# Retention attention and a routed MoE on one core: drain moved behind the last gather, raw rows in the weights' buffers, expert 5's rows turned by DMA

## The chip, the core and the metric

The kernel runs on one NeuronCore of a Trainium2 chip. A core has TensorE (PE in the profile; PEld is its weight load), VectorE (DVE), ScalarE (ACT), GpSimd (POOL) and SyncE (SP, which here only issues DMAs). The time is device microseconds of one launch. Before the change it is 446.14 us, the median of three runs (442.72 to 449.33).

## What is computed

Eight batches of eight heads, 576 positions, head size 64, go through a causal retention (attention without softmax, with a decay per head). The result, 4608 rows of 512, goes through a noisy top-2 router and eight experts.

```python
# q, k, v: [8, 8, 576, 64]
scores = 1/sqrt(64) * q @ k.transpose(0, 1, 3, 2)
Dmat = where(rel >= 0, gamma[h] ** rel, 0)
x = ((scores * Dmat) @ v)            # laid out as [4608, 512]
noisy = x @ w_gate + log1p(exp(x @ w_noise)) * noise
top2, top2_w = two largest of noisy, softmax over the two
for e in range(8):                   # w1 [8, 512, 1024], w2 [8, 1024, 512]
    rows = those with e among their two
    out[rows] += top2_w * (relu(x[rows] @ w1[e]) @ w2[e])
```

## The kernel before

**A planner writes the order.** The kernel does not issue instructions as it goes. Each piece of work is an `op` of the class `Plan` (L55) with the engine or engines that may do it, a cost, a priority, the buffers that it reads and writes, and `after`, other ops that it has to follow. When all ops are recorded, `run` simulates the engines with these costs and so decides the order of each engine's instructions and which buffer of a class each tile gets; then it emits them. Costs and priorities set nothing but this order. On the chip each engine, and each DMA queue (SP's, and POOL's for gathers and scatters), goes through its list in order.

**Buffers.** They come in classes (L253 on): `big`, ten of [128, 1024] in float32; `half`, 21 of half that size; `xg`, 24 for gathered rows; `W`, three for the weights of an expert in bf16; `ps`, the eight banks of PSUM. Streams within a class (`att` for attention, `exp` for weights, `xt` for turned rows) have quotas.

**Attention.** A unit u is one batch and four heads, 16 units in all; units 4n to 4n+3 make a batch pair. `load` (L437) brings raw k, v and q rows in by SP DMAs into `big` buffers: q per unit, k and v per batch. `cast` (L475) turns them into bf16 (k on ACT or DVE, q with its decay at L498, v at L505), `tr` turns tiles by TensorE (L521), `scores`, `states` and `out_` do the retention, `tail` the last 64 positions. `route` (L711) computes the gates of a batch pair and writes its rows with their weights to a scratch array in HBM, `xd` (L874).

**Experts.** An expert has at most 1216 rows, that is ten pieces of 128 rows (the last has 64). `weights` (L906) loads an expert: experts 0 to 2 by four POOL DMAs each that cast on the way (L914, L918), held until the loads of the units 10, 15 and 15 have landed; experts 3 to 7 by SP into `big` buffers (L928 for the first matrix, L931 for the second), from where ACT or DVE cast them into `W` (L277, L279). `fetch` (L968) gathers the rows of a piece from `xd` (L981). In the late stage each gather also waits for a recent matmul, so that gathers go at TensorE's pace. The rows have then to be turned: for experts below `CROSS` TensorE transposes them, four to a piece (L1003), and ACT or DVE copies them from PSUM; for experts from `CROSS` on, in the late stage, SP issues a DMA transpose for each piece (L993).

`up` (L1043, matmuls L1058) is the first matmul for the early tiles. In the late stage `wide` (L1071, matmuls L1084) does the first matmul of a tile interleaved with the second of the tile before (`down`, L1146; short pieces L1156); ACT applies the relu (L1067). A late expert has tiles of 512, 512 and 192 columns. `finish` (L1166) evicts a result scaled by its gate (ACT L1180, DVE L1182) and scatters it to the output by an indirect DMA on POOL's queue (L1186): in the first half of each expert's row list as a write, in the rest as an accumulating scatter. Each token has two experts, so the accumulating ones must find the writes done.

**The end.** `record` (L1210) strings it all together. Ahead of the last scatters it puts a GpSimd drain, by priority:

```python
if i == len(ts) - 1:
    pl.op("POOL", 6.0, lambda _: self.nc.gpsimd.drain(), prio=pr - 6,
          after=self.scats[i - 2][:1])
```

`overflow` (L1305) is a loop for experts with too many rows; it makes no round here.

Of the kernel before, what the change touches and what calls it, by code (L numbers as in the profile page):

```python
# [8 lines left out]
F32 = mybir.dt.float32  # L9
F16 = mybir.dt.float16  # L10
BF16 = mybir.dt.bfloat16
# [6 lines left out]
P = 128  # L18
N = 4608
NCOL = N // P  # L20
E = 8
F = 1024
DM = 512
KD = DM // P
KF = F // P
# [217 lines left out]
class Kernel:  # L243
    def __init__(self, tc, ctx, src, gates, noise, w1, w2, out, xd):
        self.tc, self.nc = tc, tc.nc
        self.src, self.gates, self.noise, self.w1, self.w2, self.out = src, gates, noise, w1, w2, out
        self.xd = xd
        nc = self.nc
        self.pl = pl = Plan()
        self.cp = ctx.enter_context(tc.tile_pool(name="fix", bufs=1))  # L250
        self.ps = ctx.enter_context(tc.tile_pool(name="ps", bufs=1, space=bass.MemoryType.PSUM))
        mk = lambda n, k, sh, dt: [(self.cp.tile(sh, dt, name=f"{n}{i}"), None) for i in range(k)]
        pl.cls("big", mk("big", 10, [P, 1024], F32), exp=4, xt=3, rt=1)  # L253
        pl.cls("half", mk("half", 21, [P, 512], F32), cs=9, exp=15, xt=3, tl=6, rt=1)
# [177 lines left out]

    def inp(self, fn, t, prio, dma):

        self.inps.append(self.pl.op("SP", 0.55, fn, w=[t], prio=prio, dma=dma, after=self.inps[-5:-4]))

    def load(self, u):  # L437
        pl, nc = self.pl, self.nc
        bp, hq, b = self.unit(u)
        d = self.u[u] = {}  # L440

        if not hq:
            self.raw = {n: [pl.buf("big", "att") for c in range(2)] for n in "kv"}
        for n in "kqv":
            if n == "q":
                t = d["rawq"] = pl.buf("big", "att")
                s = self.src[n][2 * bp + b, 4 * hq:4 * hq + 4]

                for a in range(2):
                    self.inp(lambda e, s=s, t=t, a=a: nc.sync.dma_start(  # L450
                        out=t.t[a::2].rearrange("p (h x) -> p h x", h=2),
                        in_=s[2 * a:2 * a + 2, :512].rearrange("h (p r) d -> p h (r d)", r=8)), (t, a), u, 0.72)
                continue
            d["raw" + n] = self.raw[n]
            if hq and u > 1:
                continue
            h0, nh = (4 * hq, 4) if u < 2 else (0, E)
            for c, t in enumerate(self.raw[n]):
                self.inp(lambda e, n=n, t=t, c=c: nc.sync.dma_start(
                    out=t.t[:, h0 * P:(h0 + nh) * P].rearrange("p (h x) -> p h x", h=nh),  # L460
                    in_=self.src[n][2 * bp + b, h0:h0 + nh, 256 * c:256 * c + 256].rearrange("h (p r) d -> p h (r d)", r=2)),
                    (t, hq) if u < 2 else t, u, 0.24 * nh)

    def load_tail(self, bp, prio):
        pl, nc = self.pl, self.nc
        d = self.tails[bp] = {}
        for n in "kqv":
            t = d["raw" + n] = pl.buf("half", "tl")
            for b in range(2):
                self.inp(lambda e, n=n, t=t, b=b: nc.sync.dma_start(  # L470
                    out=t.t[b * HD:(b + 1) * HD].rearrange("p (h d) -> p h d", h=E),
                    in_=self.src[n][2 * bp + b, :, 512:, :].rearrange("h s d -> s h d")),
                    (t, b), prio, 0.8)

    def cast(self, u):  # L475
        pl, nc = self.pl, self.nc
        d = self.u[u]
        hq = self.unit(u)[1]
        hs = slice(4 * hq, 4 * hq + 4)
        tab, tabq = self.fixed["tab"], self.fixed["tabq"]  # L480
        bf = lambda b: b.t.bitcast(BF16)
        kn, qb, vn = (pl.buf("half", "cs") for _ in range(3))
        rk, rq, rv = d.pop("rawk"), d.pop("rawq"), d.pop("rawv")

        def k(e, c):
            i = rk[c].t.rearrange("p (g h r d) -> p g h r d", g=2, h=4, r=2)[:, hq]
            o = bf(kn).rearrange("p (r c h d) -> p c h r d", r=2, c=2, h=4)[:, c]
            if e == "ACT":
                nc.scalar.activation(o, i, Act.Copy, scale=0.125)
            elif e == "DVE":  # L490
                nc.vector.tensor_scalar_mul(o, i, 0.125)
        for c in range(2):
            pl.op({"ACT": 0.63, "DVE": 0.43}, 0, lambda e, c=c: k(e, c), r=[(rk[c], hq)], w=[(kn, c)], prio=u, port=True)

        def q(e):
            i = rq.t.rearrange("p (h r d) -> p h r d", h=2, r=8)
            o = bf(qb).rearrange("p (r h d) -> p h r d", r=8, h=2)
            self.eng(e).tensor_tensor(o, i, tabq.t[:, 2 * hq:2 * hq + 2].unsqueeze(3).to_broadcast([P, 2, 8, HD]), Alu.mult)  # L498
        pl.op({"DVE": 1.23, "POOL": 1.91} if u > 1 else {"DVE": 1.23}, 0, q, r=[rq, tabq], w=[qb], prio=u, port=True)

        def v(e, c):
            i = rv[c].t.rearrange("p (g h r d) -> p g h r d", g=2, h=4, r=2)[:, hq]
            o = bf(vn).rearrange("p (r c h d) -> p c h r d", r=2, c=2, h=4)[:, c]
            t = tab.t[:, hs, 2 * c:2 * c + 2].unsqueeze(3).to_broadcast([P, 4, 2, HD])
            self.eng(e).tensor_tensor(o, i, t, Alu.mult)  # L505
        for c in range(2):
            pl.op({"DVE": 0.69, "POOL": 1.06}, 0, lambda e, c=c: v(e, c), r=[(rv[c], hq), tab], w=[(vn, c)], prio=u, port=True)
        d.update(kn=kn, qb=qb, vn=vn)

    def tr(self, u):  # L510
# [457 lines left out]
    def fetch(self, i, t, prio):  # L968

        pl, nc = self.pl, self.nc  # L970
        e, js, early = t
# [4 lines left out]
        for x, j in zip(xg, js):  # L976
            h, n = HPE * e + j, self.size(j)
            pace = PACE if early == 3 and i > self.ne else 0.0

            def get(_, x=x, h=h, n=n, pace=pace):  # L980
                ins = nc.gpsimd.indirect_dma_start(  # L981
                    out=x.t[:n, :], out_offset=None, in_=self.xd[:rows, :], in_offset=IOff(ap=xi.t[:n, h:h + 1], axis=0),
                    bounds_check=rows - 1, oob_is_err=False)
                if pace:
                    self.tc.add_manual_dep(ins.ins, self.mm.ins.name, mybir.DependencyInfo(
                        mybir.DependencyClass.Sync, mybir.DependencyReason.DATA), reason="gathers go at TensorE's pace")
            pl.op("POOL", 1.3, get, r=[xi] + self.xd_done[early], w=[x], prio=prio, dma=0.4, pace=pace, slack=3)
        xT = pl.buf("half" if early < 3 else "big", "xt")
        w, m, off = sum(self.size(j) for j in js), len(js) * P, self.off(js)
        xv = lambda m=m: xT.t.bitcast(BF16)[:, :KD * m].rearrange("p (k s) -> p k s", k=KD)  # L990
        if e >= CROSS and early == 3:
            for s, x in enumerate(xg):
                pl.op("SP", 0.5, lambda _, s=s, x=x, n=self.size(js[s]): nc.sync.dma_start_transpose(  # L993
                    out=xv()[:, :, off[s]:off[s] + n], in_=x.t[:n, :DM // 2].bitcast(BF16)),
                    r=[x], w=[(xT, s)], prio=prio, dma=1.1)
        for c in range(0, 0 if e >= CROSS and early == 3 else len(js), 2):
            p = self.psum("xt")
# [168 lines left out]
    def finish(self, i, t, s, prio):  # L1166
# [43 lines left out]
    def record(self):  # L1210
# [59 lines left out]
        for i in range(ne, len(ts) + 1):  # L1270
# [145 lines left out]
```

## Time and profile before

| what | value |
|---|---|
| median of three runs | 446.14 us (449.33, 442.72, 446.14) |
| profiled execution | 442.35 us |
| its span (first to last instruction) | 440.8 us |
| mean granted TensorE clock | 0.952 |
| TensorE busy | 379.5 us (86%) |
| ACT, POOL, DVE busy | 266.2, 296.9, 157.0 us |
| moved by DMA | 93.01 MB, 211 GB/s on average |
| gathers (L981), scatters (L1186) | 80 and 74 on POOL |
| TensorE transposes of gathered rows (L1003) | 240 |
| DMA transposes (L993) | 20 |

A row of the timeline gives the start, the duration, the engine, the line, the operation with output and input, and in brackets the idle time ahead of it with what ended that. A row of a window gives the busy time of PE, PEld, DVE, ACT and POOL with the count of instructions, then the granted clock of TensorE as a share of full speed, the busy share of the DMA engines and GB/s. A row of the waits gives who waited, for whom, and us in total, times and the longest. The tenths are the span in 40 slices of 11 us. Columns x elements stand behind an operation as output and input.

### The profile page before, as it was taken

The page shows a single profiled execution, that of the slowest core. Times are in us where ns is not written, and L with a number is a line of the kernel's source. Part 1 is how long each engine was busy: PE and PEld are TensorE (multiplying, and loading weights), DVE is VectorE, ACT ScalarE, POOL GpSimd, SP SyncE. Part 2 cuts the span into 40 slices and gives each one's busy share as a digit, 9 for nine tenths or more (in the row PEclk, how much of TensorE's full clock was granted, in tenths as well). Part 3 has the DMA queues.
Part 4 walks back from the last instruction along what each step waited for, and adds up shares of the span by engine and source line. Part 5 has one row for each costly group of instructions (what it writes and reads, how often), then busy time and mean ns, then how long its engine had stood idle before and what let it go on. Part 6 is the DMA issues. An engine that isn't in the chain of part 4 may idle for free. (4 is left out here: it accounts for less than half of the span.)

```text
span 440.8 us, 11068 instructions
## 1 busy us (share of the span) xinstructions
PE 379.5 (86%) x4315; PEld 243.6 (55%) x4352; DVE 157.0 (36%) x426; ACT 266.2 (60%) x458; POOL 296.9 (67%) x340
## 2 busy tenths in 40 slices
PE   2786775697699879899999799999999999999990
PEld 1675664575577657666566445555554454454450
DVE  4645689897357755101245014014113000000000
ACT  4688795855869655457657365556557555555550
POOL 8774685691888567277577577777788788562274
PEclk9999897969879889999999899999999999999996
DMA  8998999999992999964798859968779999682566
GB/s 241 311 270 192 309 252 308 321 204 210 285 273 50 246 184 202 356 230 133 226 321 317 257 170 237 292 177 238 201 168 271 204 148 150 103 101 34 66 79 103
DMA packets 94776, 93.01 MB, mean 211 GB/s; under 512 B 31615, under 2 KB 72064, under 8 KB 94722
## 3 DMA queue, kind: packets, MB, share of 16 engines
q1 hardware_dynamic: 76930, 56.83, 44.8%
q0 software_dynamic: 17792, 35.46, 39.8%
q8 instruction: 34, 0.56, 0.6%
q14 instruction: 20, 0.16, 0.1%
HBM read 72.32 MB, written 26.36 MB: 224 GB/s over the span
## 5 line engine op out<-in xcount | busy, mean ns | idle before, releaser
L1146 PE MATMUL ps<-W,half 128*128 128x512 bf16 x550 | 181.6, 381 | 3.7 <-DMA W<-in_moe_w_dram 2.5
L1084 PE MATMUL ps<-big,W 128*128 128x512 bf16 (+4 forms) x629 | 179.0, 329 | 0.8
L1067 ACT ACTIVATE half<-ps 128x512 bf16<-128x512 f32 (+5 forms) x186 | 92.9, 503 | 99.2 <-PE ps L1084 82.0
L1186 POOL DMA_INDIRECT out_dram<-half,xg x74 | 98.5, 1332 | 55.1 <-ACT half L1180 25.5
L981 POOL DMA_INDIRECT xg<-xd,xi x80 | 83.6, 1046 | 54.7 <-DMA xd<-xg 16.8
L1146 PEld LDWEIGHTS <-half 128*128 128x128 bf16 x576 | 56.0, 98 | 63.2 <-issue 3.8
L1084 PEld LDWEIGHTS <-W 128*128 128x128 bf16 x640 | 62.7, 98 | 47.2 <-issue 0.9
L1180 ACT ACTIVATE half<-ps,xg 128x512 f32<-128x512 f32 (+1 forms) x67 | 44.1, 658 | 13.7 <-PE ps L1146 10.8
L560 DVE TENSOR_TENSOR half<-ps,mask 128x512 bf16<-128x512 f32 x64 | 40.2, 679 | 15.6 <-PE ps L552 14.4
L277 ACT ACTIVATE half<-ps 128x1024 bf16<-128x1024 bf16 (+1 forms) x36 | 35.4, 999 | 15.9 <-PE ps L1003 5.9
L279 DVE CAST W<-big 128x1024 bf16<-128x1024 f32 x30 | 19.9, 719 | 55.3 <-PE ps L1156 28.7
L1182 DVE TENSOR_SCALAR half<-ps,xg 64x256 f32<-64x256 f32 (+1 forms) x15 | 9.0, 603 | 81.1 <-ACT half L1067 68.1
L505 POOL TENSOR_TENSOR half<-big,tab 128x512 bf16<-128x512 f32 x31 | 32.1, 1049 | 2.0 <-PE ps L521 1.1
L1058 PE MATMUL ps<-half,W 128*128 128x256 bf16 (+1 forms) x288 | 31.6, 267 | 2.0 <-DMA W<-in_moe_w_dram 1.7
L498 POOL TENSOR_TENSOR half<-big,tabq 128x1024 bf16<-128x1024 f32 x13 | 24.7, 1903 | 7.4 <-DMA big<-in_q_dram 4.5
L1058 PEld LDWEIGHTS <-W 128*128 128x128 bf16 x288 | 25.1, 102 | 7.0 <-DMA W<-in_moe_w_dram 2.0
L277 ACT ACTIVATE tb<-ps 64x512 bf16<-64x512 f32 x32 | 18.9, 591 | 13.4 <-PE ps L585 11.4
L277 ACT ACTIVATE xT<-ps 128x512 bf16<-128x512 f32 (+1 forms) x40 | 20.1, 555 | 7.5 <-PE ps L701 5.3
L1003 PE MATMUL ps<-ident__61,xg 128*128 128x128 bf16 (+1 forms) x240 | 19.9, 223 | 4.2 <-DMA xg<-xd,xi 4.2
L585 PE MATMUL ps<-half,half 64*64 64x64 bf16 (+2 forms) x512 | 19.6, 228 | 1.9 <-DVE half L560 1.6
L1003 PEld LDWEIGHTS <-xg 128*128 128x128 bf16 (+1 forms) x240 | 15.1, 100 | 10.7 <-DMA xg<-xd,xi 5.4
L277 ACT ACTIVATE xg<-ps 128x1024 bf16<-128x1024 bf16 (+1 forms) x20 | 17.9, 946 | 4.9 <-DMA xd<-xg 4.3
(164 smaller groups left out, 401.9 us busy)
## 6 DMA issues: line engine op xcount, KB each, us to landing
big<-in_moe_w_dram SPq DMA_DIRECT2D x40, 512.0 KB, 7.7
big<-in_q_dram SPq DMA_DIRECT2D x32, 256.0 KB, 6.6
big<-in_k_dram SPq DMA_DIRECT2D x14, 512.0 KB, 6.7
big<-in_v_dram SPq DMA_DIRECT2D x14, 512.0 KB, 8.2
W<-in_moe_w_dram POOLq DMA_DIRECT2D x12, 512.0 KB
xd<-xg SPq DMA_DIRECT2D x16, 264.0 KB, 5.7
xg<-xd,xi POOLq DMA_INDIRECT x80
out_dram<-half,xg POOLq DMA_INDIRECT x74
```

The lines of the kernel that those rows point to most:

```text
L277: self.nc.scalar.activation(out, in_, Act.Copy)
L498: self.eng(e).tensor_tensor(o, i, tabq.t[:, 2 * hq:2 * hq + 2].unsqueeze(3).to_broadcast([P, 2, 8, HD]), Alu.mult)
L505: self.eng(e).tensor_tensor(o, i, t, Alu.mult)
L560: nc.vector.tensor_tensor(S.t.bitcast(BF16).rearrange("p (h c x) -> p h c x", h=2, c=2)[:, h], p[h].t.rearrange("p (c x) -> p c x", c=2), ...
L981: ins = nc.gpsimd.indirect_dma_start(out=x.t[:n, :], out_offset=None, in_=self.xd[:rows, :], in_offset=IOff(ap=xi.t[:n, h:h + 1], axis=0), ...
L1003: nc.tensor.transpose(pv()[:, di, a:a + n], xb[:, di * P:(di + 1) * P], ident.t[:n, :n])
L1058: nc.tensor.matmul(pv()[:, f2, :], lhsT=w.t[:, o:o + P], rhs=xv()[:, di, :n], start=(di == 0), stop=(di == KD - 1))
L1067: self.nc.scalar.activation(o, i, Act.Relu)
L1084: self.mm = nc.tensor.matmul(p.t[:, :n], lhsT=w.t[:, o:o + P], rhs=xv()[:, di, :n], start=(di == 0), stop=(di == KD - 1))
L1146: self.mm = self.nc.tensor.matmul(po.t, lhsT=hv[:, c:c + P], rhs=self.W[e].t[:, o:o + DM], start=(f == 0), stop=(f == KF - 1))
L1180: nc.scalar.activation(y.t[:n, c], x, Act.Copy, scale=g()[:n])
L1186: ins = nc.gpsimd.indirect_dma_start(out=self.out[:, :], out_offset=IOff(ap=ix()[:n], axis=0), in_=y.t[:n, :], in_offset=None, bounds_chec ...
```

## The change

Four things change.

1. `CROSS` goes from 6 to 5: expert 5's ten late pieces too are turned by SP's DMA transposes, and the planner takes 2.0 instead of 0.5 for one.
2. Raw k and v rows of the batch pairs 0 and 2 go into parts of the weight buffers W1 and W2, raw q rows of the units below 8 into parts of W0, seen as float32; the rest stay in `big`, which now consists of five tiles of two. k and v of a whole batch pair share their tiles. The weights of experts 0, 1 and 2 also wait for all work on these parts.
3. The planner's cost of an accumulating scatter goes from 1.3 to 1.8.
4. The drain follows the last gather (`self.got`) by its `after`, with an earlier priority and cost 8.8 instead of 6.0.

The core of the diff:

```diff
-CROSS = 6
+CROSS = 5
...
-        pl.cls("big", mk("big", 10, [P, 1024], F32), exp=4, xt=3, rt=1)
+        bs = [self.cp.tile([P, 2, 1024], F32, name=f"big{i}") for i in range(5)]
+        pl.cls("big", [(x[:, i, :], x) for x in bs for i in range(2)], exp=4, xt=3, rt=1)
...
-        pl.cls("W", mk("W", 3, [P, KD * F + KF * DM], BF16))
+        ws = [self.cp.tile([P, KD * F + KF * DM], BF16, name=f"W{i}") for i in range(3)]
+        pl.cls("W", [(x, None) for x in ws])
+        part = lambda x, i, n: x[:, 2 * i * n:2 * i * n + 2 * n].bitcast(F32)
+        pl.cls("wkv", [(part(x, i, 2048), None) for x in ws[1:] for i in range(2)])
+        pl.cls("wq", [(part(ws[0], i, 1024), None) for i in range(4)])
...
-        if not hq:
-            self.raw = {n: [pl.buf("big", "att") for c in range(2)] for n in "kv"}
+        if u % 4 == 0:
+            self.raw = {n: [pl.buf("big", "att", 2) if bp % 2 else pl.buf("wkv", "att") for c in range(2)] for n in "kv"}
...
-                t = d["rawq"] = pl.buf("big", "att")
+                t = d["rawq"] = pl.buf("wq", "att") if u < 8 else pl.buf("big", "att")
...
-            pl.op("POOL", 1.3, get, r=[xi] + self.xd_done[early], w=[x], prio=prio, dma=0.4, pace=pace, slack=3)
+            self.got = pl.op("POOL", 1.3, get, r=[xi] + self.xd_done[early], w=[x], prio=prio, dma=0.4, pace=pace, slack=3)
...
-                pl.op("SP", 0.5, lambda _, s=s, x=x, n=self.size(js[s]): nc.sync.dma_start_transpose(
+                pl.op("SP", 2.0, lambda _, s=s, x=x, n=self.size(js[s]): nc.sync.dma_start_transpose(
...
-            self.scats.setdefault(i, []).append(pl.op("POOL", 1.3, lambda _: scat(second, True), r=[y] + src + rd,
+            self.scats.setdefault(i, []).append(pl.op("POOL", 1.8, lambda _: scat(second, True), r=[y] + src + rd,
...
-            self.weights(e, 40 + e, True, landed(u))
+            raw = (("wkv", "att"), ("wq", "att"))[e == 0]
+            self.weights(e, 40 + e, True, landed(u) + [o for b in pl.fifo[raw] for o in b.ops])
...
-                pl.op("POOL", 6.0, lambda _: self.nc.gpsimd.drain(), prio=pr - 6, after=self.scats[i - 2][:1])
+                pl.op("POOL", 8.8, lambda _: self.nc.gpsimd.drain(), prio=pr - 20, after=[self.got])
```

More of the change, by code (lines that the diff above doesn't have):

```diff
@@ L433, in inp @@
     def inp(self, fn, t, prio, dma):
-        self.inps.append(self.pl.op("SP", 0.55, fn, w=[t], prio=prio, dma=dma, after=self.inps[-5:-4]))
+        self.inps.append(self.pl.op("SP", 0.55, fn, w=t, prio=prio, dma=dma, after=self.inps[-5:-4]))
     def load(self, u):
@@ L451, in load @@
                         out=t.t[a::2].rearrange("p (h x) -> p h x", h=2),
-                        in_=s[2 * a:2 * a + 2, :512].rearrange("h (p r) d -> p h (r d)", r=8)), (t, a), u, 0.72)
+                        in_=s[2 * a:2 * a + 2, :512].rearrange("h (p r) d -> p h (r d)", r=8)), [(t, a)], u, 0.72)
                 continue
             d["raw" + n] = self.raw[n]
-            if hq and u > 1:
+            if u % 4 == 3 or bp and u % 4 == 1:
                 continue
-            h0, nh = (4 * hq, 4) if u < 2 else (0, E)
+            m = slice(u % 4 * 4, 16 if u % 4 == 2 else 8 if bp or u else 4)
             for c, t in enumerate(self.raw[n]):
[L459 to L462, printed above, removed]
+                w = [(t, x) for x in range(m.start // 4, m.stop // 4)]
+                self.inp(lambda e, n=n, t=t, c=c, m=m, bp=bp: nc.sync.dma_start(
+                    out=rows(t, m),
+                    in_=self.src[n][2 * bp:2 * bp + 2].rearrange("b h s d -> (b h) s d")[
+                        m, 256 * c:256 * c + 256].rearrange("h (p r) d -> p h (r d)", r=2)),
+                    w, u, 0.22 * (m.stop - m.start))
     def load_tail(self, bp, prio):
@@ L472, in load_tail @@
                     in_=self.src[n][2 * bp + b, :, 512:, :].rearrange("h s d -> s h d")),
-                    (t, b), prio, 0.8)
+                    [(t, b)], prio, 0.8)
     def cast(self, u):
@@ L477, in cast @@
         d = self.u[u]
-        hq = self.unit(u)[1]
+        bp, hq, bt = self.unit(u)
+        x4 = 2 * bt + hq
+        flat = lambda t: t.t.rearrange("p b x -> p (b x)") if t.n == 2 else t.t
         hs = slice(4 * hq, 4 * hq + 4)
@@ L492, in cast @@
         for c in range(2):
-            pl.op({"ACT": 0.63, "DVE": 0.43}, 0, lambda e, c=c: k(e, c), r=[(rk[c], hq)], w=[(kn, c)], prio=u, port=True)
+            pl.op({"ACT": 0.63, "DVE": 0.43}, 0, lambda e, c=c: k(e, c), r=[(rk[c], x4)], w=[(kn, c)], prio=u, port=True)
         def q(e):
@@ L506, in cast @@
         for c in range(2):
-            pl.op({"DVE": 0.69, "POOL": 1.06}, 0, lambda e, c=c: v(e, c), r=[(rv[c], hq), tab], w=[(vn, c)], prio=u, port=True)
+            pl.op({"DVE": 0.69, "POOL": 1.06}, 0, lambda e, c=c: v(e, c), r=[(rv[c], x4), tab], w=[(vn, c)], prio=u, port=True)
         d.update(kn=kn, qb=qb, vn=vn)
```

6 lines of the change are left out of this document (4 added, 2 removed).

## The prediction, made before the result

> **What bounds the kernel now.** I read the page first (busy times, slices), then windows of the span, then the waits of TensorE behind 185 us.
>
> ```profile
> span 440.8 us, 11068 instructions
> PE 379.5 (86%) x4315; PEld 243.6 (55%) x4352; DVE 157.0 (36%) x426; ACT 266.2 (60%) x458; POOL 296.9 (67%) x340
> PE   2786775697699879899999799999999999999990
> DMA  8998999999992999964798859968779999682566
> ```
>
> ```profile
> 80.00:100.00 20.00, 14.27 (x288) 11.92 (x286) 18.64 (x38) 11.95 (x21) 17.33 (x27) 0.83 1.11 259
> 180.00:200.00 20.00, 19.84 (x166) 13.72 (x168) 1.00 (x2) 11.10 (x19) 12.22 (x12) 1.00 0.77 277
> 240.00:260.00 20.00, 17.24 (x94) 8.85 (x94) 4.31 (x11) 9.66 (x19) 12.35 (x12) 0.91 0.79 261
> 400.00:420.00 20.00, 19.89 (x110) 9.76 (x110) 0.96 (x2) 10.55 (x19) 6.07 (x4) 1.00 0.35 44
> 420.00:440.80 20.80, 9.21 (x66) 5.21 (x65) 0.00 (x0) 5.40 (x13) 12.25 (x8) 0.81 0.72 96
> ```
>
> ```profile
> PE ps L1003 <- DMA xg<-xd,xi: 2.7, 1, 2.7
> ```
>
> Columns of a window: PE, PEld, DVE, ACT and POOL busy, TensorE's clock, DMA share, GB/s. There are three regimes. Up to about 180 us (attention, routing, first tiles) PE has holes while the DMA digits stand at 8 or 9: the inputs set the pace as much as any engine. From 180 to 420 us TensorE alone is the bound, 19.84 to 19.89 of 20 us, and the last fence is its only wait behind 185 us; one stretch, 240 to 260, falls to 17.24 at clock 0.91. Behind 430 us only scatters are left, on POOL. So an edit pays by fewer TensorE instructions, by closing that one hole, by a shorter end, or by earlier inputs.
>
> The profiled execution took 442.35 us, 1.55 above its span; the median of the three runs is 446.14, 3.8 more. I sum against 442.35 and add 3.8.
>
> **The drain.** POOL issues gathers and scatters in order, and the drain holds it until what it has issued is done.
>
> ```profile
> 369.88 1.05 POOL L981 DMA_INDIRECT xg<-xd,xi  x1 [0.30 <-PE ps L1156]
> 404.33 1.43 POOL L1186 DMA_INDIRECT out_dram<-half,xg  x1 [8.43 <-DVEq L1306]
> 411.26 1.54 POOL L1186 DMA_INDIRECT out_dram<-half,xg  x1 [1.79 <-ACT half L1180]
> 420.63 1.54 POOL L1186 DMA_INDIRECT out_dram<-half,xg  x1 [7.83 <-ACT half L1180]
> 431.72 1.42 POOL L1186 DMA_INDIRECT out_dram<-half,xg  x1 [0.30 <-issue]
> 433.45 1.57 POOL L1186 DMA_INDIRECT out_dram<-half,xg  x1 [0.30 <-issue]
> ```
>
> ```profile
> 413.75 0.68 ACT L1180 ACTIVATE half<-ps,xg 128x512 f32<-128x512 f32 x1
> 426.49 0.68 ACT L1180 ACTIVATE half<-ps,xg 128x512 f32<-128x512 f32 x1
> ```
>
> The bracket of the 420.63 row blames ACT, but the first eviction behind the gap was done at 414.43. The drain stood there, from 412.80 to about 420.3, 7.5 us, and the eight scatters behind it then ran back to back, 1.54+0.30 each, to 435.02. Without it the third-last scatter starts when its eviction is done, 426.49+0.68+0.30 = 427.47, the next at 429.31, the last at 431.03 (its neighbour takes 1.42+0.30) and ends at 432.60: 2.4 us sooner. The changed order puts the drain right behind the last gather and one scatter, 12 scatters from the end. In the old trace that place is the 8.43 us gap before 404.33, so 7.5 us fits there. Queued behind it are those scatters alone, no gather. The last gather itself moves later: 13 scatters from the end instead of 24; POOL has 24.7 us for 11 scatters at 1.86 and five gathers at 1.34 there, 27 us, so the drain starts some 2.5 us late, about 398, and ends about 406; by 418 the queue has caught up. Bounds: 0 (caught up too late) and -2.4; I take **-2.4**, since the gaps of 8.43 and 1.79 us together exceed the debt.
>
> **Expert 5's pieces turned by SP.** 40 of the 240 TensorE transposes go, with five PSUM copies of about 1 us on ACT or DVE, which are not the bound.
>
> ```profile
> 300.00:320.00 20.00, 2.12 (x32) 1.87 (x32) 1.00 0.78 231
> 320.00:340.00 20.00, 0.62 (x8) 0.39 (x8) 1.00 0.94 222
> DMA to landing us min/median/max: 4.1/5.2/6.0
> 326.99 0.38 PE L1084 MATMUL ps<-big,W 128*128 128x512 bf16 x1
> ```
>
> ```profile
> 247.18 0.40 PE L1003 MATMUL ps<-ident__61,xg 128*128 128x128 bf16 x4 [2.66 <-DMA xg<-xd,xi]
> 247.41 0.30 PE L1084 MATMUL ps<-big,W 128*128 128x320 bf16 x1
> ```
>
> The first two rows are windows of the transposes' line alone: expert 5's forty lie in 300 to 327, where TensorE is never idle. Four of them push the next matmul by 0.23 us (247.18 to 247.41), so ten pieces are worth 2.3 us. Bounds: -2.3, and 0 if SP delivers the pieces later than TensorE would turn them; **-2.3**, since the stage is TensorE's alone. In their place SP issues ten more DMA transposes, which land in 5.2 us (third row, of the old twenty).
>
> **Longer accumulating scatters** change the order alone: 1.8 is what the trace shows (1.54+0.30). They matter for the hole at 244:
>
> ```profile
> 239.27 1.28 POOL L981 DMA_INDIRECT xg<-xd,xi  x1 [1.23 <-PE ps L1156]
> 240.48 14.45 SPq L931 DMA_DIRECT2D big<-in_moe_w_dram  x4
> 242.11 0.30 PE L1084 MATMUL ps<-big,W 128*128 128x320 bf16 x1
> 242.46 0.30 PE L1084 MATMUL ps<-big,W 128*128 128x320 bf16 x1
> ```
>
> ```profile
> 242.00:244.00 2.00, 2.00 (x16) 1.20 (x14) 0.42 (x4) 1.20 (x3) 1.70 (x2) 1.00 0.98 365
> 248.00:250.00 2.00, 2.00 (x9) 0.90 (x8) 0.00 (x0) 1.08 (x2) 0.50 (x1) 0.63 1.09 285
> 250.00:252.00 2.00, 2.00 (x7) 0.94 (x7) 0.00 (x0) 0.74 (x2) 0.50 (x1) 0.51 0.54 162
> ```
>
> The listed order shows that the piece turned at 247.18 is the one gathered at 239.27: 7.9 us, with the weight loads beside it at 365 GB/s. The wait cost 2.66 us, and then the clock: 2x(1-0.63)+2x(1-0.51) = 1.7 us lost, 4.4 in all. How much room has each gather? I count the columns of matmuls between the one that releases a gather and its transpose, 832 columns per 0.35 us (242.11 to 242.46, one 320 and one 512 wide). Among the 15 gathers from the middle of expert 3 to the end of 4, four have under 8 us, the least 5.4, and one of the four stalled. In the changed order, where pieces are turned one by one just ahead of use, 11 of these 15 have 5.6 to 7.8 us. So the hole need not go: the pressure is wider though its worst place is milder. Bounds: -4.4 (no stall) and +8.8 (the old rate of one in four gives three); I take **0**, one stall somewhere, nearest to the one row that there is.
>
> Would a wait of 2.66 us cost any clock? The Trainium skill's "TensorE: Matmul & The Clock Gate", section "Part 1: The HAM clock gate", says that the clock halves after an idle window of about 3.4 us. By that rule the hole costs 2.7 us and not 4.4; the trace speaks against it, with 0.63 and 0.51 granted right behind the wait.
>
> **Raw rows in the weights' buffers.** The number of DMAs and their order on SP stay; buffers come free sooner.
>
> ```profile
> PE ps L521 <- POOL half L498: 3.4, 4, 1.2
> PE ps L1146 <- DMA W<-in_moe_w_dram: 2.5, 2, 1.7
> PE ps L1058 <- DMA W<-in_moe_w_dram: 1.7, 1, 1.7
> ```
>
> ```profile
> PE ps L521 <- POOL half L498: 0.5, 1, 0.5
> ```
>
> TensorE waits 3.4 us for q's casts, 0.5 of it in the first 25 us (last row, the waits of that window), where no buffer is short; 2.9 could go. But DMA stands at 1.11 in 80 to 100: rows that may start sooner need not land sooner. Against it, the weights of experts 0 to 2 now also wait for the casts out of their buffers, and TensorE already waits 2.5+1.7 for weights; these gates come after units 10 and 15 have landed, by when units 0 to 11 are long cast. Bounds: -2.9 and +4.2; I take **-1.5**, half of the gain, DMA being the cover.
>
> **Sum:** -2.4-2.3+0-1.5 = -6.2; 436.15 for the profiled execution, and with 3.8 **440.0** for the median.
>
> **Rivals.**
>
> No stall (B): the new order keeps every gather ahead. For it: the least room grows from 5.4 to 5.6 and transposes wait for one piece, not four. Another -4.4: 435.5, faster by over 2%.
>
> More stalls (C): two or three of the 11. For it: the 7.9 us landing is longer than all 11 rooms. Against it: that landing lay beside a burst of loads. +4.4 to +8.8: 444.4 to 448.8. Beside it stands the Trainium skill's "DMA: Bandwidth & Descriptors", section "Issuing engines are not separate DMA queues": DMAs of all issuers run on the same 16 engines and interleave. By that rule the ten new transposes would slow gathers too; the late gather beside SP's loads agrees.
>
> Late weights (D): +4.2 in place of -1.5 makes 445.7.
>
> Slower (E): SP's queue is in order. In the changed order the first two transposes of expert 5 stand ahead of expert 6's last four weight loads and the other eight behind. The waits of SP's queue in 260 to 335, and its rows:
>
> ```profile
> SPq L931 <- PE ps L1146: 12.6, 2, 11.1
> SPq L931 <- DVE W L279: 10.7, 3, 10.1
> ```
>
> ```profile
> 280.56 11.45 SPq L931 DMA_DIRECT2D big<-in_moe_w_dram  x3
> 315.06 4.06 SPq L993 DMA_TRANSPOSE big<-xg  x2
> 324.52 3.74 SPq L931 DMA_DIRECT2D big<-in_moe_w_dram  x4
> ```
>
> Those loads were held 11.1 and 10.1 us and ended at 292.0. If the holds return behind expert 5's first transposes and last beyond 326.99-5.2 = 321.8, TensorE waits up to 21.2 us: 461.2. Against it: expert 6's pair of 315.06 had its loads behind it with no long hold (324.52, done in 3.74), and there are 30 us of room.
>
> **Chances.** Forecast 0.36 (own range 437.5 to 443), B 0.34, C 0.14, D 0.06, E 0.10. Over 2% faster (below 437.2, about what a measurement can tell from no change) is B, 0.34; within 2% are the forecast, C and D, 0.56; slower E, 0.10. The range leaves E out and the outer ends of B and C: 431 (B with the rows' full 2.9, and 3 more of the runs' spread) to 449 (C).
>
> **What would show it.** Drain: its gap lies ahead of the 12th-last scatter, and the last scatter ends some 2.4 us behind the last eviction or less. Transposes: 200 TensorE and 30 SP ones, none of them waited for at expert 5. Gathers: the waits of TensorE behind 185 us, one of 2 to 3 us with a cold clock behind it; none is B, two or three C. Rows: the waits for q's casts fall below 3.4 while those for weights stay at 4.2. A wait of TensorE on turned pieces at expert 5 would be E. I am wrong if the stage from 180 to 420 us gains or loses anything that is not a wait for gathered rows.

## The result, and the profile after

Over 20 runs each, the changed kernel takes 440.29 us (436.12 to 445.22) against 444.38 (441.06 to 449.33) for the kernel before, a ratio of 0.9895 with a 95% interval of 0.9862 to 0.9928: 1.1% faster, a gain clear of the noise, but inside the 2% that the chances spoke of. All ratios, here and below, leave out executions that took over 1.5% more than the fastest one of the same kernel (in the run after3 below that leaves three of six). The profiled execution took 438.85 us, its span 437.2.

First the page of the changed kernel (span, busy times, the slices).

```profile
span 437.2 us, 11020 instructions
PE 378.9 (87%) x4312; PEld 240.4 (55%) x4312; DVE 161.9 (37%) x425; ACT 263.3 (60%) x450; POOL 298.1 (68%) x344
PE   2787686585989699999899898999999899999991
DMA  8997999999993999973689859459999999697586
```

The late stage, before a row of nines with one seven, now has four eights, and the DMA share from the first wide matmul to the last eviction goes from 0.77 to 0.84. To see what moved, cut both executions at three marks: the first matmul of the late stage, the end of the last eviction, the end of the last scatter. The first mark is the first start in the line of the wide matmuls (changed kernel's line numbers are 12 higher in this part of the code), here before and after:

```profile
L1084 PE MATMUL ps<-big,W x629: 243/379/474, 202.7 to 426.0; 128*128 128x512 bf16 x78, 128*128 128x192 bf16 x48, 128*128 128x384 bf16 x16, 128*128 128x448 bf16 x8
```

```profile
L1096 PE MATMUL ps<-big,W x640: 243/370/390, 199.1 to 424.6; 128*128 128x512 bf16 x80, 128*128 128x192 bf16 x48, 128*128 128x384 bf16 x16, 128*128 128x448 bf16 x8
```

The last eviction and the scatters around it, after:

```profile
427.98 0.69 ACT L1192 ACTIVATE half<-ps,xg 128x512 f32<-128x512 f32 x1 [0.92 <-ACT half L1192]
```

```profile
396.90 1.58 POOL L1198 DMA_INDIRECT out_dram<-half,xg  x1 [0.30 <-issue]
406.00 1.54 POOL L1198 DMA_INDIRECT out_dram<-half,xg  x1 [7.51 <-ACT half L1079]
429.69 1.56 POOL L1198 DMA_INDIRECT out_dram<-half,xg  x1 [0.30 <-POOLq L1319]
```

| stretch | before | after | difference |
|---|---|---|---|
| start to first wide matmul | 202.7 | 199.1 | -3.6 |
| from there to the end of the last eviction (429.99; 428.67) | 227.3 | 229.6 | +2.3 |
| from there to the end of the last scatter (435.02; 431.25) | 5.0 | 2.6 | -2.4 |
| from there to the end | 5.8 | 5.9 | +0.2 |

(Before, the last eviction started at 429.30 and took 0.69.) So there are two gains, at the start and at the end, and a loss in between. The drain is the gap of 7.51 us ahead of 406.00, behind the last gather and one scatter, as planned, and the last scatter now ends 2.6 us behind the last eviction.

The waits of TensorE in the changed kernel behind 185 us, then two rows of its waits over the whole span:

```profile
PE ps L1015 <- DMA xg<-xd,xi: 4.8, 5, 1.5
PE ps L1158 <- ACT half L1079: 2.6, 1, 2.6
```

```profile
PE ps L533 <- POOL half L510: 7.2, 5, 3.0
PE ps L1158 <- DMA W<-in_moe_w_dram: 0.2, 1, 0.2
```

One wait of 2.7 us for gathered rows has become five of up to 1.5, and there is a new one of 2.6 us for a relu on ACT. The waits for q's casts rose from 3.4 to 7.2 us, but that is no work of the change: a second profile of each kernel (before2 and after2 below) has 6.0 and 6.6. Those for the weights of the early experts fell from 4.2 to 0.2 (3.3 to nothing in the second pair).

The new wait is a short story on ACT's list (rows of ACT, then of TensorE):

```profile
346.83 0.58 ACT L1079 ACTIVATE half<-ps 128x512 bf16<-128x512 f32 x1
349.25 1.06 ACT L282 ACTIVATE W<-big 128x1024 bf16<-128x1024 f32 x1 [1.84 <-DMA big<-in_moe_w_dram]
350.21 1.07 ACT L1079 ACTIVATE half<-ps 128x512 bf16<-128x512 f32 x2
```

```profile
350.84 0.39 PE L1158 MATMUL ps<-W,half 128*128 128x512 bf16 x1 [2.61 <-ACT half L1079]
```

Between two relus (L1079) stands a cast of expert 7's weights (L282) whose load has not landed; ACT waits 1.84 us for it, casts, and only then does the relu that TensorE wants. Over the late stage ACT waits so four times, which it never did before; and the slowest weight load took 16.6 us to land instead of 11.8 (rows of the changed kernel's waits of ACT behind 195 us and of its weight loads, then of the loads before):

```profile
ACT W L282 <- DMA big<-in_moe_w_dram: 6.1, 4, 2.3
```

```profile
DMA to landing us min/median/max: 3.9/7.3/16.6
```

```profile
DMA to landing us min/median/max: 4.1/7.7/11.8
```

### The profile page after: what moved, and what is told of

It reads as the page before. It is cut to its first block, busy times and chain, and to the rows that moved or that the text cites. A ratio compares the mean times of both kernels' runs of the same rounds, so it can differ in the third digit from the quotient of the medians.

```text
span 437.2 us, 11020 instructions
## 1 busy us (share of the span) xinstructions
PE 378.9 (87%) x4312; PEld 240.4 (55%) x4312; DVE 161.9 (37%) x425; ACT 263.3 (60%) x450; POOL 298.1 (68%) x344
## 5 line engine op out<-in xcount | busy, mean ns | idle before, releaser
L1158 PE MATMUL ps<-W,half 128*128 128x512 bf16 x576 | 186.2, 379 | 2.9 <-ACT half L1079 2.6
L1096 PE MATMUL ps<-big,W 128*128 128x512 bf16 (+4 forms) x640 | 182.5, 329 | 0.0
L1079 ACT ACTIVATE half<-ps 128x512 bf16<-128x512 f32 (+5 forms) x188 | 93.5, 504 | 95.3 <-PE ps L1096 79.9
L1192 ACT ACTIVATE half<-ps,xg 128x512 f32<-128x512 f32 (+1 forms) x58 | 39.3, 678 | 12.9 <-PE ps L1158 11.6
L1194 DVE TENSOR_SCALAR half<-ps,xg 64x256 f32<-64x256 f32 (+1 forms) x24 | 14.0, 591 | 89.1 <-ACT half L1079 40.5
L282 ACT ACTIVATE half<-ps 128x1024 bf16<-128x1024 bf16 (+1 forms) x35 | 34.8, 1011 | 12.3 <-PE ps L533 4.9
L284 DVE CAST W<-big 128x1024 bf16<-128x1024 f32 x25 | 17.2, 735 | 64.6 <-PE ps L1168 28.9
L282 ACT ACTIVATE tb<-ps 64x512 bf16<-64x512 f32 x32 | 18.9, 591 | 15.1 <-PE ps L597 14.9
L282 ACT ACTIVATE xT<-ps 128x512 bf16<-128x512 f32 (+1 forms) x37 | 18.6, 553 | 9.8 <-PE ps L642 6.7
L1015 PE MATMUL ps<-ident__61,xg 128*128 128x128 bf16 (+1 forms) x200 | 17.6, 219 | 4.8 <-DMA xg<-xd,xi 4.8
L533 PE MATMUL ps<-ident__61,half 128*128 128x128 bf16 x128 | 12.5, 255 | 10.2 <-POOL half L510 7.2
L564 PE MATMUL ps<-half,half 64*64 64x128 bf16 x512 | 12.9, 244 | 9.1 <-ACT half L282 8.8
L1015 PEld LDWEIGHTS <-xg 128*128 128x128 bf16 (+1 forms) x200 | 13.0, 98 | 12.5 <-DMA xg<-xd,xi 5.3
L597 PEld LDWEIGHTS <-half 64*64 64x64 bf16 (+1 forms) x512 | 16.6, 123 | 5.7 <-issue 3.6
```

Of the source, the lines that this page charges most:

```text
L282: self.nc.scalar.activation(out, in_, Act.Copy)
L284: self.eng(e).tensor_copy(out, in_)
L597: nc.tensor.matmul(o[h * HD:(h + 1) * HD, hp, n, :], lhsT=kk[:k, r, c, y], rhs=vv[:k, r, c, y].unsqueeze(1).to_broadcast([k, n.stop - n.st ...
L1015: nc.tensor.transpose(pv()[:, di, a:a + n], xb[:, di * P:(di + 1) * P], ident.t[:n, :n])
L1079: self.nc.scalar.activation(o, i, Act.Relu)
L1096: self.mm = nc.tensor.matmul(p.t[:, :n], lhsT=w.t[:, o:o + P], rhs=xv()[:, di, :n], start=(di == 0), stop=(di == KD - 1))
```

## The experiments

Twelve runs, on chips 6, 3 and 2, which are of two kinds: on chip 3, as in the result above, the kernel before takes 444 us, on chips 6 and 2 it takes 459. Ratios are always to the kernel before, run beside it on the same chip; first wide, rows (waits of TensorE for gathered rows behind the first wide matmul, us and times) and tail (end of the last eviction to end of the last scatter) are from each one's profile.

| kernel | chip's before | ratio (95%) | first wide | rows | tail |
|---|---|---|---|---|---|
| changed | 444.4 | 0.9895 (0.9862 to 0.9928) | 199.1 | 4.8, 5 | 2.6 |
| after2: changed, again | 444.2 | 0.9881 (0.9843 to 0.9920) | 199.3 | 4.2, 5 | 2.6 |
| before2: before, again | 444.2 | | 207.2 | 1.6, 2 | 5.0 |
| o_scat: only the scatters' cost | 444.2 | 0.9961 (0.9925 to 0.9997) | 204.3 | 1.0, 2 | 5.1 |
| c_dve: changed, weight casts on DVE | 444.2 | 1.0130 (1.0072 to 1.0188) | 200.6 | 5.3, 4 | 2.6 |
| after3: changed, again | 459.2 | 0.9761 (0.9646 to 0.9875) | 206.5 | 4.7, 4 | 2.6 |
| o_raw: only the raw rows | 459.2 | 0.9781 (0.9718 to 0.9843) | 206.8 | 2.8, 3 | 5.0 |
| u_scat: changed, scatters' cost old | 458.6 | 0.9793 (0.9736 to 0.9851) | 208.6 | 2.8, 3 | 2.6 |
| u_scat2: the same, again | 459.2 | 0.9793 (0.9721 to 0.9864) | 208.1 | 3.6, 4 | 2.6 |
| u_cross: changed, expert 5 by TensorE | 458.6 | 0.9815 (0.9765 to 0.9865) | 208.8 | 4.1, 4 | 2.6 |
| u_cross2: the same, again | 459.2 | 0.9775 (0.9712 to 0.9839) | 206.5 | 4.9, 4 | 2.6 |
| u_raw: changed, raw rows old | 458.6 | 0.9899 (0.9854 to 0.9945) | 216.4 | 2.6, 3 | 3.3 |
| u_drain: changed, drain old | 458.6 | 0.9929 (0.9886 to 0.9971) | 211.3 | 8.1, 5 | 5.0 |

One thing makes the column "first wide" worth more than single profiles are. For the first 215 us the traces show each engine running the same operations in the same order (TensorE by its weight loads) in all kernels with the raw rows moved, and likewise in those without (before, before2, o_scat, u_raw); only one of DVE's first instructions changes place. So the column compares two early orders. On the 444 us kind the mark lies at 202.7, 207.2 and 204.3 without the move and at 199.1, 199.3 and 200.6 with it; on the 459 us kind at 216.4 without and at 206.5 to 208.8 with it (211.3 in u_drain).

**The raw rows: u_raw.** The changed kernel with the hunks of `load`, `cast`, the classes `big`, `W`, `wkv` and `wq` and the weights' waits taken back:

```diff
-        pl.cls("wkv", [(part(x, i, 2048), None) for x in ws[1:] for i in range(2)])
-        pl.cls("wq", [(part(ws[0], i, 1024), None) for i in range(4)])
...
-            self.weights(e, 40 + e, True, landed(u) + [o for b in pl.fifo[raw] for o in b.ops])
+            self.weights(e, 40 + e, True, landed(u))
```

> The changed kernel with the raw rows back in the ten big buffers; everything else as changed. Theory A (rows): the changed kernel's first wide matmul came at 199.1 us instead of 202.7 because the weights of experts 0 to 2 no longer made TensorE wait (4.2 us before, 0.2 after). Then here it comes at about 202.5 again, TensorE waits 3 to 4 us for those weights, and the time is 3 to 4 us above the changed kernel, about 444. Theory B (spread): the 3.6 us of the early stage are the spread between executions; then the first wide matmul lies within 1.5 us of 199.1 and the time is that of the changed kernel, about 440.

The first wide matmul comes at 216.4, where u_scat and u_cross, with the raw rows moved, have 208.6 and 208.8 on the same chip, and the ratio is 0.9899 against their 0.9793 and 0.9815. So theory B falls, but the way is not theory A's: TensorE waited only 1.2 us for weights here. The size has to be taken with care too. Of the 7.8 us to u_scat, 6.0 are TensorE's own work, which took 166.7 us at a granted clock of 0.87 against 160.7 at 0.92, and the profiled execution is the longest of u_raw's six (456.24, median 453.44). The absolute times expected were those of the other kind of chip.

What moved are the loads. Here are SP's last raw loads and POOL's issues of the second weight matrices of experts 0 to 2, u_raw first and then u_scat in each pair (first and last start stand behind the durations):

```profile
L470 SPq DMA_DIRECT2D half<-in_v_dram x8: 595/615/1172, 37.8 to 136.8; - x8
```

```profile
L480 SPq DMA_DIRECT2D half<-in_v_dram x8: 595/630/1577, 36.6 to 129.7; - x8
```

```profile
L918 POOL DMA_DIRECT2D W<-in_moe_w_dram x6: 775/837/901, 95.7 to 176.9; - x6
```

```profile
L930 POOL DMA_DIRECT2D W<-in_moe_w_dram x6: 751/820/853, 95.3 to 170.8; - x6
```

The last raw load is issued 7 us sooner and the last weights 6 us sooner. The second does not simply follow from the first. Expert 2's weights are held until unit 15's loads have landed, but they are issued 20 to 40 us behind the last raw load, where POOL's list has them. In the old order all four of expert 2's loads stand behind a gather that is held; in the new one the first of them stands ahead of it (rows of POOL, before and after the change):

```profile
157.34 1.08 POOL L981 DMA_INDIRECT xg<-xd,xi  x1 [7.00 <-DMA xd<-xg]
158.43 0.75 POOL L914 DMA_DIRECT2D W<-in_moe_w_dram  x1
```

```profile
151.68 0.73 POOL L926 DMA_DIRECT2D W<-in_moe_w_dram  x1
156.71 1.09 POOL L993 DMA_INDIRECT xg<-xd,xi  x1 [4.30 <-DVE half L696]
```

**The raw rows alone: o_raw.** The same hunks put into the kernel before, all else as before.

> The kernel before with only the raw rows moved to the weights' buffers. Theory A (this part carries most of the gain): the first wide matmul comes 3 to 8 us earlier than in the kernel before, the weights of expert 2 land some 6 us earlier, and the ratio is 0.985 to 0.992. Theory B (the early gain needs the other parts): ratio 0.995 or more.

Theory A, and more than its range: 0.9781, within the intervals as much as the whole change on that chip (0.9761), with the first wide matmul at 206.8 and the last weights issued at 168.9. The kernel before has no profile on this kind of chip, so the comparison is with u_raw (216.4 and 176.9). The tail is the old 5.0 us, so this gain is of the early stage. The parts do not add up: 2.2% for the raw rows alone, 1.0% for all the rest (u_raw), 2.4% together. The intervals, up to 1.2 points to each side, leave room for that.

**The drain: u_drain.**

```diff
-                pl.op("POOL", 8.8, lambda _: self.nc.gpsimd.drain(), prio=pr - 20, after=[self.got])
+                pl.op("POOL", 6.0, lambda _: self.nc.gpsimd.drain(), prio=pr - 6, after=self.scats[i - 2][:1])
```

> The changed kernel with the drain back at its old place, eight scatters from the end. Theory A: the last scatter ends about 5.0 us behind the last eviction instead of 2.6, and the time is 2.4 above the changed kernel, about 442.7. Theory B: the 7.5 us that the drain holds POOL are hidden in both places; then the gap behind the last eviction stays at 2.6 and the time at 440.

The last eviction and the last scatter of u_drain:

```profile
453.08 0.69 ACT L1192 ACTIVATE half<-ps,xg 128x512 f32<-128x512 f32 x1 [0.82 <-PE ps L1158]
```

```profile
457.20 1.57 POOL L1198 DMA_INDIRECT out_dram<-half,xg  x1 [0.30 <-issue]
```

The tail is 458.77-453.77 = 5.0 us: theory A, and in the fourteen profiles the tail is 5.0 or 5.1 where the drain stands 8 scatters from the end, and 2.6 where it stands 10, 12 or 18 from the end (u_raw, 11 from the end, has 3.3). The ratio cannot be put down to that alone: 0.9929 against 0.9761 for the changed kernel on this kind of chip is nearly 8 us. The planner's order is no cause either: in u_drain's trace every engine runs the changed kernel's operations in the changed kernel's order, the drain apart. The profiled execution took 466.06 us, the longest of its thirteen, so that only its tail is used here, and the runs of this kernel spread over 14 us. The changed kernel itself did not run on this chip. That rest stays open.

**The scatters' cost: u_scat, u_scat2 and o_scat.**

```diff
-            self.scats.setdefault(i, []).append(pl.op("POOL", 1.8, lambda _: scat(second, True), r=[y] + src + rd,
+            self.scats.setdefault(i, []).append(pl.op("POOL", 1.3, lambda _: scat(second, True), r=[y] + src + rd,
```

> The changed kernel with the accumulating scatters planned at 1.3 again. In its order 7 instead of 11 of the 15 gathers have under 8 us to their transposes, the least 5.2, and the drain stands 18 scatters from the end. Theory A (the longer scatters in the order shorten the gathers' room, and that is what TensorE waits for): its waits for gathered rows behind 185 us fall from 4.8 in five places to at most 3 in two or three, and the time falls by 1 to 3 us, to about 438. Theory B (the room is not what decides, but the weight loads beside the gather): 4 to 5 us of waits as before and 440.

> The changed kernel with accumulating scatters planned at 1.3 again, a second time, now beside the changed kernel on one chip. Theory A (the longer scatters in the order cost TensorE's waits for gathered rows): 1 to 3 us below the changed kernel, waits for rows 2 to 3 us against 4 to 5. Theory B (they cost nothing): within 1 us of the changed kernel; the first reading of 0.9793 was the other chip.

o_scat is the reverse, 1.8 put into the kernel before.

> The kernel before with the accumulating scatters planned at 1.8 and nothing else. Its last gather moves to 13 scatters from the end and 11 of the 15 gathers have under 8 us. Theory A: more waits for gathered rows (4 to 8 us behind the start of the late stage) and no gain, ratio 1.00 to 1.01. Theory B: the better planned scatters give TensorE fewer waits, ratio 0.99 or less.

With the raw rows moved, the old cost gives 2.8 to 3.6 us of waits for rows instead of 4.2 to 4.8, the way theory A has it, but u_scat has a further 1.1 us at a transpose which the profile puts to issue. The time does not follow: 0.9793 twice, against 0.9761 (0.9646 to 0.9875) for the changed kernel, whose six runs there lie between 443.8 and 455.2. And alone (o_scat) the cost shortens the rooms nearly as much: in its trace 11 of the same 15 gathers start under 8 us ahead of their transposes (13 in the changed kernel, 5 before), yet TensorE waits only 1.0 us for rows and the kernel is 0.4% faster than before. So short room as such does not make the stalls: theory A of o_scat falls. Its ratio of 0.9961 is neither theory's, and the part's own worth is between nothing and 0.4% as far as these runs tell.

**The transposes: u_cross, u_cross2.**

```diff
-CROSS = 5
+CROSS = 6
...
-                pl.op("SP", 2.0, lambda _, s=s, x=x, n=self.size(js[s]): nc.sync.dma_start_transpose(
+                pl.op("SP", 0.5, lambda _, s=s, x=x, n=self.size(js[s]): nc.sync.dma_start_transpose(
```

> The changed kernel with expert 5's pieces turned by TensorE again (240 transposes, 20 of SP). Theory A (price of the transposes by DMA): TensorE has 2.3 us more to do, but the hole of 2.6 us at 348, where ACT stood behind a cast of weights that had not landed, is gone, since the DMA engines carry ten transposes less beside those loads; the time stays within 1 us of the changed kernel's 440.3. Theory B (the hole has another cause and the transposes are a pure gain): the hole stays and the time is 442.6.

> The changed kernel with expert 5's pieces turned by TensorE, a second time, beside the changed kernel on one chip. Theory A (the transposes by DMA give TensorE 2.3 us and take part of it back by late loads): 0 to 2 us above the changed kernel, its late stage without waits 1.5 to 2.3 us longer. Theory B (pure loss by contention): below the changed kernel.

The window of the late stage (first wide matmul to end of the last) in u_cross2 and in after3, on one chip:

```profile
206.50:434.60 228.10, 223.12 (x1383) 117.70 (x1380) 39.77 (x81) 129.59 (x234) 154.82 (x127) 1.00 0.79 186
```

```profile
206.50:432.80 226.30, 220.94 (x1343) 115.60 (x1340) 36.60 (x76) 129.21 (x234) 154.91 (x127) 1.00 0.85 193
```

TensorE's busy time differs by 2.2 us with 40 matmuls, so the saving is real, and the window is 1.8 us shorter, so little of it is taken back. The DMA share goes from 0.79 to 0.85 for it. In the ratios it is lost in the spread (0.9775 and 0.9761). The waits of ACT for weight loads are there without the ten transposes too: 4.1 us in u_cross and 1.6 in u_cross2, so the transposes are not their sole cause. They come with any of the new orders: 1.9 us in o_scat and 1.8 in o_raw, where one other part alone is changed, and none in before and before2. Theory A's account of the hole at 348 is not shown.

**ACT's list: c_dve.** Only the engine of the weights' casts changes:

```diff
-            pl.op({"ACT": 1.06, "DVE": 0.7}, 0, lambda g, k=k, t=t: self.copy(g, w.t[:, k * F:(k + 1) * F], t.t), hold=1,
+            pl.op({"DVE": 0.7}, 0, lambda g, k=k, t=t: self.copy(g, w.t[:, k * F:(k + 1) * F], t.t), hold=1,
```

> The changed kernel with the casts of experts 3 to 7's weights planned on DVE alone (before: on ACT or DVE, whichever the planner takes; 15 of 40 fell to ACT). Theory A (ACT's list is in order: a relu stands behind a cast whose load has not landed, and TensorE behind the relu): TensorE's waits of its second matmul for the relu vanish, 2.6 us in the changed kernel's profile, and the time is 2 to 3 us below the changed kernel. Theory B (DVE now blocks its own evictions and the gates in the same way): TensorE waits as long for something on DVE, no gain.

The waits of DVE behind 195 us in c_dve, and those of TensorE behind 188 us:

```profile
DVE W L284 <- DMA big<-in_moe_w_dram: 45.6, 11, 13.3
```

```profile
PE ps L1015 <- DMA xg<-xd,xi: 5.3, 4, 2.3
PE ps L1096 <- DMA big<-xg: 2.6, 1, 2.6
PE ps L1096 <- ACT half L1192: 2.0, 1, 2.0
```

The wait of the second matmul for the relu is not there, as theory A said; but the changed kernel itself has none either in after2, its profile on this chip, so that this tells little. The kernel is 1.3% slower than before, 2.5% slower than the changed one. The planner re-ordered the whole late stage around it: DVE now waits 45.6 us for loads, and TensorE 2.6 us for a DMA transpose and 2.0 for an eviction. There is no gain, as theory B has it, and the loss goes beyond it.

**The yardsticks: after2, before2, after3.**

> The changed kernel itself beside the other runs of this call, since the first four ran on a chip where the kernel before takes 458.6 us and not 444.4. Theory A: its ratio to before is again 0.985 to 0.993, the first wide matmul comes some 3 to 4 us earlier than in the kernel before of this call, and TensorE again waits for ACT's relu, with ACT waiting for late weight loads ahead of it, and for gathered rows, 5 to 9 us together. Theory B: the ratio and the early gain belong to one chip and come out within 0.5% of 1.

> The kernel before, for its profile on this chip. Theory A: one stall of 2 to 3 us for gathered rows behind the start of the late stage, no wait of ACT for weight loads, about 4 us of waits for the weights of experts 1 and 2. Theory B: the same waits for ACT as in the changed kernel, so that they belong to the chip and not to the change.

> The changed kernel as the yardstick of this call, since its ratios of 0.9895 and 0.9881 come from a chip where the kernel before takes 444 us, while the four kernels with one part undone ran where it takes 458.6. Theory A (one price for each part, whatever the chip): 0.985 to 0.993 again. Theory B (the change is worth more where DMA is slower): on a chip with 455 us or more before, 0.98 or less.

after2 repeats the result. Against before2 its first wide matmul comes 7.9 us earlier (199.3, 207.2); it has no relu wait behind that mark and two waits of ACT for loads, 2.1 us, where before2 has none. So the hole of 2.6 us at 348 does not come in every execution. after3's 0.9761 leans to the numbers of theory B: where the kernel before takes 459 us the change gains twice as much, and by o_raw in the early stage. The intervals of 0.9881 and 0.9761 overlap, though, and that a slower DMA is the reason is not shown. With the raw rows moved, the profiles of the 459 us kind (u_drain left aside) are about as far at 160 us as those of the 444 us kind, with 345 to 379 matmuls to go against 344 to 352; from there to the first wide matmul they take 46.5 to 48.8 us instead of 39.1 to 40.6, with the DMA engines less busy (0.73 to 0.79 against 0.87 to 0.91). What holds them there is open.

## Why the prediction was right, and where not

The forecast of 440.0 is met by 440.29, but the closeness is luck, since two errors cancel. The sum of -6.2 was to bring the profiled execution to 436.15 us; it took 438.85, 2.7 more. The 3.8 us between the profiled execution and the median came from three runs; in the result it is 1.4 (440.29 less 438.85), 2.4 less. The gain itself was forecast at 6.2 us and is 4.1 between the medians of 20 runs, 3.5 between the two profiled executions. Inside the sum, too, the terms err both ways.

**Right: the drain.** -2.4 forecast; the tail went from 5.03 to 2.58 us, -2.45, and it is 2.6 in every profile with the new drain but u_raw's (3.3). The place, the 7.5 us and the catching up behind it are as worked out: the gap runs from 398.48 to 406.00. One count was off without consequence: the old trace has 23 scatters behind the last gather, not 24.

**Right: the transposes.** -2.3 forecast from four transposes pushing the next matmul by 0.23 us; 2.2 us measured in busy time (u_cross2 against after3), 1.8 in the window. Rival E did not appear: no wait of TensorE for turned pieces in the changed kernel.

**Half right: the gathered rows.** I took 0, one stall of the old kind. The profile has five short ones, 4.8 us together, and none with a cold clock behind it: +2.1 for the waits and -1.7 for the clock make +0.4. Near enough in sum, but the step behind it failed: I read the risk from the room under 8 us, and o_scat, with 11 such gathers, waits 1.0 us. What turns a short room into a wait (with the raw rows moved there are 2.8 to 5.3 us of waits, without that 1.0 to 2.7, u_drain aside) is open.

**Mis-sized: the raw rows.** I took -1.5, half of the 2.9 us that TensorE waited for q's casts, with DMA as the cover, and held that the weights' waits would stay. The first wide matmul came 3.6 us earlier in the first pair of profiles and 7.9 in after2 against before2, and on the slower chip the raw rows alone gave 0.9781. Over the three profiles with and the three without the move on the 444 us kind, the mark comes 5.0 us earlier in the mean (199.7 against 204.7); the kernel before alone moves by 4.5 between two executions, so that the 3.6 of one pair is no exact size. The size did not come through q's casts, whose waits differ as much between executions. It was the loading that moved. The windows from the start to the first wide matmul, before and after:

```profile
0.00:202.70 202.70, 156.86 (x2964) 125.31 (x2977) 120.23 (x350) 135.04 (x219) 137.86 (x210) 0.92 0.95 245
```

```profile
0.00:199.10 199.10, 157.52 (x2973) 124.92 (x2974) 124.90 (x349) 131.78 (x215) 140.74 (x215) 0.91 0.97 250
```

TensorE is as busy in both, and the DMA share goes from 0.95 to 0.97. "Rows that may start sooner need not land sooner" was the step that failed: the 1.11 of one window is not the whole stage, and SP's queue did wait for buffers ahead of the raw rows of `load`, 18.2 us in before2 and 9.1 in after2 (sums over the rows of its waits). The last raw load is issued at 130.0 and 130.5 us (after, after2) instead of 130.8 and 134.3 (before, before2), the last weights of expert 2 at 167.2 and 167.7 instead of 170.3 and 174.3, and the 4.2 and 3.3 us that TensorE waited for weights fall to 0.2 and nothing. How much of this comes from earlier loads and how much from expert 2's new place in POOL's list no run separates.

**Missed: the relu behind a late load.** +2.6 in the profile of the result, in none of my rivals. By its own last sentence the prediction is wrong here: the stage from 180 to 420 us lost something that is no wait for gathered rows. The wait is absent behind the same mark in after2 and after3 and there in u_scat (2.8), u_scat2 (2.5), u_raw (3.1) and u_drain (4.8 in three): the same program has it in one execution and not in another, so it seems to hang on when single loads land.

The sum for the pair of profiles: -3.6 (early), -2.4 (tail), -2.2 (transposes), +0.4 (rows), +2.6 (relu), +0.2 (end) make -5.0; measured -3.6 in span. The 1.4 us left lie in the late stage, and no row names them. TensorE's busy time there cannot decide it (222.6 us before, 221.3 after): records are missing, 1355 and 1343 matmuls where the second should have 40 fewer.

## What to carry to other kernels

Where an early stage has holes in its engines and DMA stands at 0.95, look at who holds the loads back before calling DMA the bound: buffers that stand idle until later (here those of the weights) are room for raw inputs, and what queues behind the inputs moves with them. A blocking operation on an in-order queue costs nothing in a gap that is there anyway: find the gap in the trace, put the operation behind the last instruction that something urgent waits for, and check that the debt is worked off before the end. A cast that waits for a DMA can hold up the engine whose next instruction the bottleneck needs (1.84 us on ACT became 2.61 on TensorE), but moving it to another engine through a planner moves everything else as well. And two executions of one program can differ by more than a part of the change is worth: compare all profiles that share an order, not one pair.

## What the runs showed of the hardware

Whether a wait of TensorE costs clock is not a matter of its length alone at this size. The wait of 2.66 us before the change had granted clocks of 0.63 and 0.51 in the two 2 us stretches from 248 on. The one of 2.61 us in the changed kernel has none (three windows from 348 on; TensorE is idle until 350.84), while one of 3.14 us in u_raw, up to 366.31, has again (three windows from 364 on). And one of 2.80 us in u_scat, longer than the one that cost clock before the change, has none (the wait, then three windows from 324 on):

```profile
348.00:350.00 2.00, 0.24 (x2) 0.00 (x0) 0.00 (x0) 0.75 (x1) 1.70 (x2) 1.00 1.09 119
350.00:352.00 2.00, 1.14 (x7) 0.55 (x8) 0.00 (x0) 2.00 (x6) 0.45 (x1) 1.00 1.09 240
352.00:354.00 2.00, 2.00 (x16) 1.18 (x14) 0.00 (x0) 1.19 (x5) 1.57 (x1) 1.00 1.21 225
```

```profile
364.00:366.00 2.00, 0.00 (x0) 0.00 (x0) 0.00 (x0) 1.28 (x2) 0.46 (x1) 1.00 1.08 134
366.00:368.00 2.00, 1.69 (x7) 0.94 (x8) 0.00 (x0) 1.85 (x5) 0.89 (x1) 0.66 1.24 239
368.00:370.00 2.00, 2.00 (x8) 0.95 (x7) 0.00 (x0) 0.33 (x1) 1.70 (x2) 0.50 1.39 171
```

```profile
327.33 0.39 PE L1158 MATMUL ps<-W,half 128*128 128x512 bf16 x1 [2.80 <-ACT half L1079]
```

```profile
324.00:326.00 2.00, 0.54 (x4) 0.17 (x2) 0.48 (x1) 0.27 (x1) 1.69 (x2) 1.00 1.32 111
326.00:328.00 2.00, 0.67 (x5) 0.44 (x6) 0.00 (x0) 1.91 (x5) 0.30 (x2) 1.00 1.12 350
328.00:330.00 2.00, 2.00 (x16) 1.18 (x14) 0.00 (x0) 0.90 (x3) 1.04 (x1) 1.00 1.07 365
```

Where a wait does cost clock it is about 1.7 us. This fits the Trainium skill's "TensorE: Matmul & The Clock Gate", section "Part 1: The HAM clock gate", in that an activity window of fixed length decides and not the wait itself; by its figure of about 3.4 us neither 2.66 nor 3.14 should have been enough, and the runs show that they were, so the figure is not a safe floor.

The drain holds POOL longer than its DMAs run. Before the change the last scatter ahead of it ends at 412.80 and POOL goes on at about 420.3; in these two windows of that hold the DMA engines move next to nothing:

```profile
416.00:418.00 2.00, 2.00 (x14) 1.09 (x12) 0.00 (x0) 1.22 (x3) 0.00 (x0) 1.00 0.00 0
418.00:420.00 2.00, 2.00 (x15) 1.19 (x14) 0.00 (x0) 1.19 (x3) 0.00 (x0) 1.00 0.04 8
```

So over 4 of the 7.5 us are the drain's own, with no DMA of POOL's queue left to run. The gap at the drain is 7.0 to 7.8 us in thirteen profiles, at four different places, and 8.3 in c_dve.

Chips of two kinds ran the same kernel 3% apart (444 and 459 us), and the change was worth 1.1 to 1.2% on one and 2.4% (1.2 to 3.5) on the other.
